# Attention into a bilinear MLP on one core: the order of one transpose, and of two exponentials behind a copy

## The chip, the cores and the metric

The kernel runs on one core of a Trainium2 chip. The metric is the device time of the whole program in microseconds. Times are medians of several executions; the profile is of one further execution with the hardware profiler.

## The reference

Two stages are chained. Both work in float32 (the MLP weights come as float64 and are converted).

```python
# attention, B=8 batches, H=8 heads, S=512 tokens, Ns=32 state rows, D=64
scores  = x @ state.T / 8;  a  = softmax(scores,  over the 32 state rows);  xread = a  @ state
scores2 = state @ x.T / 8;  a2 = softmax(scores2, over the 512 tokens);     sread = a2 @ x
y = concat([xread, sread], tokens).reshape(B * (S + Ns), H * D)
# MLP without activations
out = (((y @ w1) * (y @ w2)) @ w3) @ w_out
```

Both softmaxes read the same scores, once in each direction: for the token reads a maximum over 32 state rows belongs to each token, for the state reads a maximum over 512 tokens belongs to each state row.

## The kernel before

**Tiles.** The scores of a batch are computed with the 8 x 32 state rows of all heads on the partitions: a PSUM tile of 128 x 2 x 512 (two banks, `per_head` at line 148, called by `scores` at line 183). The hidden layer of a batch has eight tiles of 128 features (`ft` 0 to 7). For each, `stage1_sums` (line 320) makes 12 matmuls of 512 columns into a PSUM tile of two banks; ScalarE copies the first bank to SBUF (line 524) and VectorE multiplies the copy with the second bank (line 403, in `hidden_quarters`). All of these two-bank tiles, those of the scores among them, come from one pool, `ps_2`, with three buffers. A matmul group that takes a buffer waits until everything that reads its former content is done.

**Order in a batch.** `quarter_batch(b)` runs the hidden layer of batch b and, beside it, the softmaxes of batch b+1. TensorE's order is written by hand: tiles 0 and 1, then the last piece of state weights (line 148), the state read of batch b (line 252), the scores of batch b+1 (line 148), then tiles 2 to 7, and then the products of the second layer (lines 434 to 451). With three buffers in turn, tile 4 takes the buffer of the scores, so it waits for all that reads them.

**What reads the scores** is in `scores` (lines 180 to 206):
- `turn`, line 191: VectorE transposes the whole tile in blocks of 32 x 32 into SBUF, for the softmax over state rows. That goes on with a maximum (line 213), a subtraction (line 214) and an exponential (line 217) on the SBUF copy.
- `maxima`, lines 194 and 195: VectorE takes the maximum of each row over the 512 tokens, then multiplies the small result (128 x 2) with -1/8.
- the exponentials, line 204: ScalarE, one for each of the two banks, with the scaled maxima as bias and the row sums accumulated; each is followed by a short instruction that reads the accumulator.

For batches above `PLAIN` (= 1) the program traces maxima first, then the transpose; for batches 0 and 1 the other way round.

**What sets the order of the engines.** TensorE and SyncE issue in program order throughout, ScalarE and VectorE only in the prologue, to which the softmaxes of batch 0 belong (they end in lines 626 to 630). Everywhere else a planner orders ScalarE and VectorE at compile time: it walks through a modelled time and gives a free engine the ready instruction that comes first by priority (program order; what stands under `high_priority`, the copies of line 524 and the products of line 403, goes before the rest). On the chip each engine then works its list strictly in that order. `tc.issue_after(i)` adds an order to the plan: what its block traces on the engine of `i` is queued behind `i`. It adds no wait on other engines.

The planner also sets the waits between engines. For PSUM it keeps instructions of two engines on the same bank apart, also when both only read it. In the program as compiled, the first exponential of batch 2 waits for the count that the transpose of batch 2 raises, though it uses nothing that the transpose makes. Batch 2 is the only batch whose transpose stands behind the scaled maxima in VectorE's list; in batches 3 to 7 the multiplication stands last, and the exponential waits for its count.

The calls in `quarter_batch` that drive this, at tile 2:

```python
            elif ft == 2:
                next(softmax, None)
                with tc.issue_after(q["whole"].ins):
                    next(softmax, None)
```

The first `next` traces the transpose, the maxima and the exponentials, the second lines 213 to 217, which stand on VectorE behind the product of tile 2 (line 403).

Of the kernel before, what the change touches and what calls it, by code (L numbers as in the profile page):

```python
# [36 lines left out]
PLAIN = 1  # L37

@with_exitstack
def attn_bilinear_kernel(  # L40
# [10 lines left out]
    nc = tc.nc  # L51
# [10 lines left out]
    SCALE = 1.0 / math.sqrt(D)  # L62
# [26 lines left out]
    def bank():  # L89
        return ps_o.tile([P, NF], F32, name="ps_o")  # L90

    def two_banks():
        return ps_2.tile([P, 2, NF], F32, name="ps_2")

    def split(hi, lo, src):

        return (
            nc.scalar.copy(out=hi, in_=src),  # L98
            nc.vector.tensor_tensor(out=lo, in0=src, in1=hi.bitcast(F32), op=ALU.subtract),  # L99
        )  # L100
# [41 lines left out]
    def per_head(ps, b, moving):  # L142


        for j in range(NP):
            for q in range(KT):
                rows = slice(q * D, (q + 1) * D)
                nc.tensor.matmul(  # L148
                    ps[j * NS:(j + 1) * NS, q], sts[b][rows, j], moving(rows, j), start=True, stop=True
                )  # L150
# [14 lines left out]
    def work_tile():  # L165
        return att.tile([P, KT, S], F32, name="work")

    def move_blocks(dest, src):

        for j in range(NP):  # L170
            for c in range(P // NS):
                nc.sync.dma_start(
                    out=dest(slice(c * NS, (c + 1) * NS), j), in_=src(slice(j * NS, (j + 1) * NS), c)
                )

    def attention_steps(b):
        xd = x_tiles[b]
        a2 = {}

        def scores():  # L180

            ps = two_banks()
            per_head(ps, b, lambda rows, j: xd[rows, j])
            yield
            flat = lambda t: t.rearrange("p k s -> p (k s)")

            s1 = work_tile()
            m2 = att.tile([P, KT], F32, name="m2")

            def turn():  # L190
                nc.vector.transpose(out=flat(s1), in_=flat(ps))

            def maxima():
                nc.vector.tensor_reduce(out=m2, in_=ps, axis=AX.X, op=ALU.max)
                nc.vector.tensor_scalar_mul(m2, m2, -SCALE)

            for step in (maxima, turn) if b > PLAIN else (turn, maxima):
                step()
            e2 = att.tile([P, KT, S], F32, name="e2", bufs=1)
            sum2 = att.tile([P, KT], F32, name="sum2")  # L200
            a2["e"], a2["sum"] = e2, sum2
            for kt in range(KT):
                one = slice(kt, kt + 1)
                nc.scalar.activation(  # L204
                    out=e2[:, kt], in_=ps[:, kt], func=AF.Exp, bias=m2[:, one], scale=SCALE, accum_out=sum2[:, one]
                )
            if b > PLAIN:
                yield

            J = KT * S // NS  # L210
            s1v = flat(s1).rearrange("p (j n) -> p j n", n=NS)
            m1 = att.tile([P, J], F32, name="m1")
            nc.vector.tensor_reduce(out=m1, in_=s1v, axis=AX.X, op=ALU.max)
            nc.vector.tensor_tensor(
                out=s1v, in0=s1v, in1=m1.unsqueeze(2).broadcast_to([P, J, NS]), op=ALU.subtract
            )
            nc.scalar.activation(out=s1, in_=s1, func=AF.Exp, scale=SCALE)
            yield
            nc.vector.tensor_scalar_add(sum2, sum2, 1e-9)
            nc.vector.reciprocal(out=sum2, in_=sum2)  # L220
            sum1 = att.tile([P, J], F32, name="sum1")
            nc.vector.tensor_reduce(out=sum1, in_=s1v, axis=AX.X, op=ALU.add)
            nc.vector.tensor_scalar_add(sum1, sum1, 1e-9)
            nc.vector.reciprocal(out=sum1, in_=sum1)
            nc.vector.tensor_tensor(
                out=s1v, in0=s1v, in1=sum1.unsqueeze(2).broadcast_to([P, J, NS]), op=ALU.mult
            )
            yield
            at = work_tile()
            nc.vector.transpose(out=flat(at), in_=flat(s1))  # L230
            at_tiles[b] = [att.tile([P, KT, S], F32R, name=f"at_{part}", bufs=1) for part in ("hi", "lo")]
            last = split(*at_tiles[b], at)
            yield

            blocks = work_tile()
            with tc.issue_after(last[1].ins):
                nc.vector.transpose(out=flat(blocks), in_=flat(e2))
            a2["t"] = work_tile() if b < PLAIN else att.tile([P, KT, S], F32, name="e2", bufs=1)
            tiles = lambda t: t.rearrange("p k (t m) -> p (k t) m", m=P)
            move_blocks(lambda its, j: tiles(a2["t"])[its, :, j * NS:(j + 1) * NS],  # L240
                        lambda mine, c: tiles(blocks)[mine, :, c * NS:(c + 1) * NS])

        def read_state():

            xs = token_tiles[b]

            ps = (bank() if b else two_banks()[:, 0])[:, :KT * D].rearrange("p (k d) -> p k d", k=KT)
            for kt in range(KT):
                for t in range(NT):
                    for j in range(NP):  # L250
                        mine = slice(j * NS, (j + 1) * NS)
                        nc.tensor.matmul(  # L252
                            ps[mine, kt], a2["t"][:, kt, t * P + j * NS:t * P + (j + 1) * NS],
                            xs[:, t, 2 * j + kt], start=(t == 0), stop=(t == NT - 1),
                        )
            scaled = att.tile([P, KT, D], F32, name="scaled", bufs=1)
            a2["read"] = nc.vector.tensor_tensor(
                out=scaled, in0=ps, in1=a2["sum"].unsqueeze(2).broadcast_to([P, KT, D]), op=ALU.mult
            )
            turned = att.tile([P, KT, D], F32, name="turned")  # L260
            nc.vector.transpose(
                out=turned.rearrange("p k d -> p (k d)"), in_=scaled.rearrange("p k d -> p (k d)")
            )
            yield
            move_blocks(lambda its, j: sread[its, j, b * NS:(b + 1) * NS],
                        lambda mine, c: turned.rearrange("p k (c n) -> p (k c) n", n=NS)[mine, c])

        return scores, read_state, a2


# [40 lines left out]
    def stage1_sums(b, ft):  # L311
        half, c = divmod(ft * P, NF)
        ps = two_banks()
        hi, lo = at_tiles[b]
        for i in range(2):
            w_hi, w_lo = sw_tiles[b][half, i]
            k = 0
            for kt in range(KT):
                for w, a in ((w_hi, lo), (w_hi, hi), (w_lo, hi)):
                    nc.tensor.matmul(  # L320
                        ps[:, i], w[:, kt, c:c + P], a[:, kt], start=(k == 0), stop=(k == 3 * KT - 1)
                    )
                    k += 1
        return ps
# [59 lines left out]
    def tmp_tile():  # L384
        return main.tile([P, NF], F32, name="tmp", bufs=4)
# [131 lines left out]
    def quarter_batch(b):  # L517
        q = {"raw": []}
        softmax = iter(())
        for ft in range(FT):  # L520
            ps = stage1_sums(b, ft)
            a_sb = tmp_tile()
            with tc.high_priority():
                nc.scalar.copy(out=a_sb, in_=ps[:, 0])  # L524
            hidden_quarters(a_sb, ps[:, 1], ft, q)
            if ft == 1:
                run([*late_units, reads[b]])
                if b + 1 < B:
                    scores, reads[b + 1], _ = attention_steps(b + 1)
                    softmax = scores()  # L530
                    next(softmax)
                    load_tokens(b + 1)
                if b + 2 < B:
                    load_x(b + 2)
            elif ft == 2:
                next(softmax, None)
                with tc.issue_after(q["whole"].ins):
                    next(softmax, None)
            elif ft == 4:
                next(softmax, None)  # L540
            if b == PLAIN and ft == 1:
                combine_weights(QF - 1)
        units = sw_steps(b + 1) if b + 1 < B else []
        late_units[:] = units[3:]
        stage2_quarters(b, q, units[:3], [lambda: softmax])

    def run(steps):
        for step in steps:
            for _ in step() or ():
                pass  # L550


    with tc.tile_pool(name="pro", bufs=2) as pro:
# [62 lines left out]
        softmax = scores()  # L616
# [136 lines left out]
```

## Time and profile before

| | |
|---|---|
| median of 3 runs | 497.06 us (496.87 to 497.6) |
| the profiled execution | 496.86 us, span of its instructions 495.1 us |
| around the span | 1.76 us |
| TensorE busy | 483.6 us (98% of the span) |
| VectorE busy | 389.6 us (79%) |
| ScalarE busy | 236.0 us (48%) |
| mean granted TensorE clock | 0.999 |

The profile names an instruction by line, engine (PE TensorE matmul, PEld its weight load, DVE VectorE, ACT ScalarE, SP SyncE), operation and tiles. In the timeline a row has its start, its duration, and in brackets the idle time of its engine ahead of it with what ended that. Starts are in microseconds from the start of the span. Instructions of one engine are pipelined, so that the next one can start a little before the end of the one ahead; what a chain pays for an instruction is mostly the distance from start to start.

### The profile page before, as it was taken

What the parts mean: (1) busy time and instruction counts of PE and PEld (TensorE: products, weight loads), DVE (VectorE), ACT (ScalarE), POOL (GpSimd) and SP (SyncE); (2) the same over time, 40 slices, a digit from 0 to 9 for tenths busy, and PEclk for the clock granted to TensorE, in tenths of its full rate; (3) what the DMA queues carried; (4) which work ended last, traced back from release to release, by engine and by line L of the source; (5) the groups of instructions that cost most, each with busy time, mean ns of one, the idle gap of its engine ahead of it and who ended that gap; (6) DMA issues with size and microseconds to landing.
All of it is one profiled execution on the core that took longest, in us unless ns stands there. A gap on an engine that the chain in (4) does not pass through costs nothing.

```text
span 495.1 us, 8617 instructions
## 1 busy us (share of the span) xinstructions
PE 483.6 (98%) x3390; PEld 368.8 (74%) x3390; DVE 389.6 (79%) x576; ACT 236.0 (48%) x364; POOL 0.2 (0%) x4
## 2 busy tenths in 40 slices
PE   8999999999999999999999999999999999999996
PEld 5444467767788868886888688767976797899885
DVE  5669896799899579958995898589858985678870
ACT  4777784454456045604560455045504551454640
POOL 0000000000000000000000000000000000000000
PEclk9999999999999999999999999999999999999999
DMA  8996971053114404130413041304130223001101
GB/s 339 363 377 235 373 277 28 16 218 61 34 42 164 105 4 177 41 89 5 177 41 90 5 178 43 86 5 178 44 86 5 88 44 85 6 3 42 44 1 44
DMA packets 56361, 52.49 MB, mean 106 GB/s; under 512 B 42752, under 2 KB 50944, under 8 KB 51712
## 3 DMA queue, kind: packets, MB, share of 16 engines
q1 hardware_dynamic: 47488, 43.27, 26.3%
q10 hardware_dynamic: 8832, 8.65, 5.1%
q8 instruction: 27, 0.44, 0.4%
q14 instruction: 14, 0.11, 0.1%
HBM read 38.27 MB, written 8.91 MB: 95 GB/s over the span
## 4 chain that ended last, share of the span: by engine, by line
PE 88%; ACT 4%; DVE 3%; issue 3%; DMA 1%; ACTq 0%; DVEq 0%
PE ps L320 32%; PE ps_o L434 11%; PE ps L446 8%; PE ps L148 7%; PE ps_o L334 7%; PE ps_o L439 5%; PE ps L451 4%; PE ps L691 3%; PE ps_o L584 3%; PE ps_o L571 3%; PE ps L571 3%; PE ps L693 2%; PE ps_o L252 1%; ACT e L204 1%; DMA raw<-in_w_k_dram 1%
## 5 line engine op out<-in xcount | busy, mean ns | idle before, releaser
L320 PE MATMUL ps<-at_lo,sw_hi 128*128 128x512 f32 x256 | 101.9, 398 | 4.8 <-ACT e L204 4.8
L320 PE MATMUL ps<-at_hi,sw_hi 128*128 128x512 f32 x256 | 99.9, 390 | 0.0
L320 PE MATMUL ps<-at_hi,sw_lo 128*128 128x512 f32 x256 | 99.8, 390 | 0.0
L524 ACT COPY tmp<-ps 128x512 f32<-128x512 f32 x56 | 32.8, 585 | 112.9 <-PE ps L320 101.5
L320 PEld LDWEIGHTS ps<-at_lo,sw_hi 128*128 128x128 f32 x256 | 48.1, 188 | 22.9 <-ACT e L204 7.3
L320 PEld LDWEIGHTS ps<-at_hi,sw_lo 128*128 128x128 f32 x256 | 48.1, 188 | 10.2
L320 PEld LDWEIGHTS ps<-at_hi,sw_hi 128*128 128x128 f32 x256 | 48.1, 188 | 9.6 <-issue 0.2
L403 DVE TENSOR_TENSOR g_x<-tmp,ps 128x512 f32<-128x512 f32 x28 | 19.2, 686 | 34.6 <-ACT tmp L524 34.6
L462 DVE TENSOR_TENSOR tmp<-tmp,ps 128x512 f32<-128x512 f32 x42 | 28.9, 687 | 19.0 <-PE ps L451 18.1
L99 DVE TENSOR_TENSOR sw_lo<-ps,sw_hi 128x1024 fp32r<-128x1024 f32 (+1 forms) x34 | 38.3, 1147 | 1.5 <-ACT sw_hi L98 1.5
L98 ACT CAST g_hi<-raw 128x512 fp32r<-128x512 f32 x42 | 24.5, 618 | 16.9 <-DVE raw L403 9.1
L98 ACT CAST g_hi<-g_x 128x512 fp32r<-128x512 f32 x42 | 26.0, 622 | 12.4 <-PE ps_o L434 6.3
L434 PEld LDWEIGHTS ps_o<-t,g_hi 128*128 128x128 f32 x224 | 27.7, 191 | 5.5 <-issue 5.0
L148 PE MATMUL ps<-w_sb,st 64*32 64x512 f32 (+1 forms) x544 | 31.4, 571 | 0.0
L98 ACT CAST sw_hi<-ps 128x1024 fp32r<-128x1024 f32 (+1 forms) x34 | 31.1, 966 | 0.5 <-PE ps L148 0.5
L434 PE MATMUL ps_o<-t,g_hi 128*128 128x256 f32 x224 | 29.8, 286 | 0.3 <-ACT tmp L482 0.3
L99 DVE TENSOR_TENSOR g_lo<-raw,g_hi 128x512 fp32r<-128x512 f32 x42 | 28.2, 685 | 1.9 <-PE ps_o L439 1.6
L434 PE MATMUL ps_o<-wo,g_hi 128*128 128x256 f32 x224 | 29.1, 283 | 0.0
L434 PEld LDWEIGHTS ps_o<-wo,g_hi 128*128 128x128 f32 x224 | 28.3, 192 | 0.5
L584 PE MATMUL ps_o<-w_sb,w 128*128 128x512 f32 x64 | 28.5, 599 | 0.0
L99 DVE TENSOR_TENSOR g_lo<-g_x,g_hi 128x512 fp32r<-128x512 f32 x42 | 27.1, 681 | 1.8 <-PE ps_o L439 1.8
L446 PE MATMUL ps<-t,g_hi 128*128 128x512 f32 x112 | 28.1, 393 | 0.0
(103 smaller groups left out, 784.7 us busy)
## 6 DMA issues: line engine op xcount, KB each, us to landing
raw<-in_w_k_dram SPq DMA_DIRECT2D x8, 1024.0 KB, 6.9
x_d<-in_x_d_dram SPq DMA_DIRECT2D x8, 1024.0 KB, 7.2
raw<-in_w_dram SPq DMA_DIRECT2D x8, 1024.0 KB, 6.2
x_s<-in_x_s_dram SPq DMA_DIRECT2D x8, 1024.0 KB, 5.0
out_dram<-tmp ACTq DMA_DIRECT2D x56, 128.0 KB, 1.9
raw<-in_w3t_dram SPq DMA_DIRECT2D x4, 1024.0 KB, 7.2
e<-work SPq DMA_DIRECT2D x112, 32.0 KB, 2.0
sread<-turned SPq DMA_DIRECT2D x128, 4.0 KB, 1.7
```

Of the source, the lines that this page charges most:

```text
L98: nc.scalar.copy(out=hi, in_=src),
L99: nc.vector.tensor_tensor(out=lo, in0=src, in1=hi.bitcast(F32), op=ALU.subtract),
L148: nc.tensor.matmul(ps[j * NS:(j + 1) * NS, q], sts[b][rows, j], moving(rows, j), start=True, stop=True)
L320: nc.tensor.matmul(ps[:, i], w[:, kt, c:c + P], a[:, kt], start=(k == 0), stop=(k == 3 * KT - 1))
L334: nc.tensor.matmul(ps[:, :DO], g, wo[w][:, ft, :], start=(ft == 0 and k == 0), stop=(ft == FT - 1 and k == 2))
L434: nc.tensor.matmul(ps[:, tt * HO:(tt + 1) * HO], g, w(part, k), start=(fresh and k == 0 and tt == 0 and part == "lo"), stop=False, skip_gr ...
L439: nc.tensor.matmul(ps[:, tt * HO:(tt + 1) * HO], g, w("hi", k), start=False, stop=(k == QF - 1), skip_group_check=True)
L446: nc.tensor.matmul(ps[:, tt].rearrange("p (n d) -> p n d", n=2), g, w(k), start=(k == 0), stop=False, skip_group_check=True,)
L462: sum2 = lambda out, x, y: nc.vector.tensor_tensor(out=out, in0=x, in1=y, op=ALU.add)
L524: nc.scalar.copy(out=a_sb, in_=ps[:, 0])
L571: nc.tensor.matmul(w34_ps[i][:, :DO], chunks[k][:, DO + i * P:DO + (i + 1) * P], w_out[k], start=(k == 0), stop=(k == FT - 1),)
L584: nc.tensor.matmul(w34_ps[i][:, :DO], w3s[i][:, k * P:(k + 1) * P], w_out[k], start=(k == 0), stop=(k == FT - 1))
```

## The change

In `scores`, the second of the two steps is queued on VectorE behind the last instruction of the first: for batches above `PLAIN` the transpose behind the scaled maxima, for batches 0 and 1 the two instructions of the maxima behind the transpose. In `quarter_batch`, what the softmax traces on ScalarE at tile 2, the two exponentials of line 204, is queued behind ScalarE's copy of that same tile, the third.

```diff
             def turn():
-                nc.vector.transpose(out=flat(s1), in_=flat(ps))
+                return nc.vector.transpose(out=flat(s1), in_=flat(ps))
 
             def maxima():
                 nc.vector.tensor_reduce(out=m2, in_=ps, axis=AX.X, op=ALU.max)
-                nc.vector.tensor_scalar_mul(m2, m2, -SCALE)
-
-            for step in (maxima, turn) if b > PLAIN else (turn, maxima):
-                step()
+                return nc.vector.tensor_scalar_mul(m2, m2, -SCALE)
+
+            first, second = (maxima, turn) if b > PLAIN else (turn, maxima)
+            with tc.issue_after(first().ins):
+                second()
...
             with tc.high_priority():
-                nc.scalar.copy(out=a_sb, in_=ps[:, 0])
+                copied = nc.scalar.copy(out=a_sb, in_=ps[:, 0])
...
             elif ft == 2:
-                next(softmax, None)
+                with tc.issue_after(copied.ins):
+                    next(softmax, None)
                 with tc.issue_after(q["whole"].ins):
                     next(softmax, None)
```

## The prediction

> **What bounds the kernel now.** I read the page's head first, then the waits of TensorE, then the timeline of the stretch in which those waits lie.
>
> ```profile
> span 495.1 us, 8617 instructions
> PE 483.6 (98%) x3390; PEld 368.8 (74%) x3390; DVE 389.6 (79%) x576; ACT 236.0 (48%) x364; POOL 0.2 (0%) x4
> ```
>
> TensorE is the engine that sets the end, and only what it waits for can be won. The view of the waits, for TensorE, is led by one line that comes back (total, times, longest):
>
> ```profile
> PE ps L320 <- ACT e L204: 4.8, 5, 1.0
> ```
>
> Five times tile 4 of the hidden layer stands still for ScalarE's exponentials, about 1 us each. The five are the same event in five batches, those that compute the scores of batches 3 to 7; I follow the first of them. TensorE's timeline there:
>
> ```profile
> 181.64 0.39 PE L320 MATMUL ps<-at_hi,sw_hi 128*128 128x512 f32 x1
> 181.87 0.39 PE L320 MATMUL ps<-at_hi,sw_lo 128*128 128x512 f32 x1
> 183.21 0.50 PE L320 MATMUL ps<-at_lo,sw_hi 128*128 128x512 f32 x1 [0.95 <-ACT e L204]
> 183.55 0.40 PE L320 MATMUL ps<-at_hi,sw_hi 128*128 128x512 f32 x1
> 183.79 0.39 PE L320 MATMUL ps<-at_hi,sw_lo 128*128 128x512 f32 x1
> 184.01 0.40 PE L320 MATMUL ps<-at_lo,sw_hi 128*128 128x512 f32 x1
> ```
>
> The step from matmul to matmul is 0.23 (181.64 to 181.87). Without a wait tile 4 would start at 182.10; it starts at 183.21, 1.11 late, and by its fourth matmul the loss is 184.01 - (182.10 + 3 x 0.23) = 1.22, since the pipe fills anew. The last batch, which has no scores to make, checks that; the chain of waits has
>
> ```profile
> 176.59 2.97 PE ps L320 x12
> 183.21 11.17 PE ps L320 x48
> 421.34 16.55 PE ps L320 x72
> ```
>
> The same 72 matmuls of tiles 2 to 7 take 16.55 there, and 183.21 + 11.17 - 176.59 = 17.79 here: 1.24 more. So the whole stall is worth 5 x 1.24 = 6.2 us, and no version of this change can win more. What keeps tile 4 waiting is read from ScalarE and VectorE:
>
> ```profile
> 181.23 0.69 ACT L204 ACTIVATE e<-ps,m 128x512 f32<-128x512 f32 x1 [4.28 <-issue]
> 181.81 0.19 ACT L204 ACTIVATION_READ_ACCUMULATOR e<-ps,m 128x1 f32 x1
> 181.90 0.57 ACT L524 COPY tmp<-ps 128x512 f32<-128x512 f32 x1
> 182.37 0.70 ACT L204 ACTIVATE e<-ps,m 128x512 f32<-128x512 f32 x1
> 182.95 0.21 ACT L204 ACTIVATION_READ_ACCUMULATOR e<-ps,m 128x1 f32 x1
> 183.04 0.59 ACT L524 COPY tmp<-ps 128x512 f32<-128x512 f32 x1
> ```
>
> ```profile
> 178.75 1.19 DVE L194 TENSOR_REDUCE m<-ps 128x2 f32<-128x1024 f32 x1
> 179.86 1.23 DVE L191 STREAM_TRANSPOSE work<-ps 128x1024 f32<-128x1024 f32 x1
> 181.01 0.13 DVE L195 TENSOR_SCALAR m<-m 128x2 f32<-128x2 f32 x1
> 182.51 0.69 DVE L403 TENSOR_TENSOR g_x<-tmp,ps 128x512 f32<-128x512 f32 x1 [1.37 <-ACT tmp L524]
> 183.12 1.21 DVE L213 TENSOR_REDUCE m<-work 128x32 f32<-128x1024 f32 x1
> 184.24 0.16 DVE L219 TENSOR_SCALAR sum<-sum 128x2 f32<-128x2 f32 x1
> 184.36 1.22 DVE L214 TENSOR_TENSOR work<-work,m 128x1024 f32<-128x1024 f32 x1
> ```
>
> The chain is: maximum (178.75), transpose (179.86), scaling (181.01), first exponential (181.23), the copy of the third tile (181.90), second exponential (182.37), end of its accumulator read (183.16), tile 4 (183.21). The scaling needs only the maximum, but stands behind the transpose. The copy has been possible since the third tile's matmuls ended, at 176.59 + 2.97 = 179.56, while ScalarE sat idle for 4.28 with the exponential at the head of its queue, and is now paid for between the two exponentials.
>
> **Part 1: the copy goes ahead of the exponentials.** ScalarE is free from 181.23 - 4.28 = 176.95, so the copy runs at about 179.6 to 180.2, in a time in which ScalarE does nothing. Between the exponentials it goes away. What two exponentials in direct succession cost stands in batch 2:
>
> ```profile
> 134.27 0.58 ACT L524 COPY tmp<-ps 128x512 f32<-128x512 f32 x1
> 134.75 0.69 ACT L204 ACTIVATE e<-ps,m 128x512 f32<-128x512 f32 x1
> 135.33 0.20 ACT L204 ACTIVATION_READ_ACCUMULATOR e<-ps,m 128x1 f32 x1
> 135.42 0.69 ACT L204 ACTIVATE e<-ps,m 128x512 f32<-128x512 f32 x1
> ```
>
> From start to start 135.42 - 134.75 = 0.67, against 182.37 - 181.23 = 1.14 now. That takes 0.47 off the path. Behind the copy on ScalarE waits nothing but the exponentials, which can't run before 181.2 anyway. The cover is wide: the copy would cost its 0.47 again only if tile 2 ended after 180.8.
>
> **Part 2: the transpose goes behind the scaling.** Here the order of start is not enough, since it matters what the exponentials wait for. Both exponentials read the banks that the transpose reads, and the planner keeps two engines off one bank: the one compiled instance of the new order, batch 2, has its exponential waiting for the transpose and not for the scaling. So I take it that the exponentials start after the transpose, now the last of the three on VectorE. Then this part doesn't win the transpose's time; it only swaps the two ends of the same chain, and costs a little, because the scaling can't be overlapped with the maximum it needs. No trace here has maximum, scaling and transpose in direct succession; batch 0 has the first two and batch 2 the last two:
>
> ```profile
> 39.33 1.19 DVE L194 TENSOR_REDUCE m<-ps 128x2 f32<-128x1024 f32 x1
> 40.55 0.17 DVE L195 TENSOR_SCALAR m<-m 128x2 f32<-128x2 f32 x1
> ...
> 133.20 0.16 DVE L195 TENSOR_SCALAR m<-m 128x2 f32<-128x2 f32 x1
> 133.27 1.25 DVE L191 STREAM_TRANSPOSE work<-ps 128x1024 f32<-128x1024 f32 x1
> ```
>
> ```profile
> 40.81 0.69 ACT L204 ACTIVATE e<-ps,m 128x512 f32<-128x512 f32 x1 [1.67 <-DVE m L195]
> ...
> 185.62 1.06 ACT L217 ACTIVATE work<-work 128x1024 f32<-128x1024 f32 x1 [1.99 <-DVE work L214]
> ```
>
> Maximum to scaling: 40.55 - 39.33 = 1.22 (lower bound 179.86 - 178.75 = 1.11, the step to an instruction that needs nothing of it). Scaling to transpose: 0.07 (upper bound 0.13, its whole duration). Transpose: 1.23 (1.25 at most). From its end to ScalarE: 185.62 - (184.36 + 1.22) = 0.04 behind a wide instruction, 40.81 - (40.55 + 0.17) = 0.09 behind the scaling; I take 0.08, nearer to the row with the same waiter. The first exponential starts at 178.75 + 1.22 + 0.07 + 1.23 + 0.08 = 181.35, between 181.20 and 181.44; now it is 181.23. So part 2 costs 0.12, at best it wins 0.03 and at worst it costs 0.21.
>
> The page "PSUM — Partial Sum Buffer" of the Trainium skill, section "PSUM bank collisions raise a hardware error", is the rule that speaks against this part: two engines on one bank and the same partitions at once are an error, ScalarE and VectorE both reading included, so software has to keep them apart. In the rows shown here no exponential overlaps its transpose, but none of them tells whether that was the wait or the queue; by this rule the sum is the one below, without it the one of the first rival.
>
> **The sum.** Second exponential 181.35 + 0.67 = 182.02; from its start to tile 4 it stays 183.21 - 182.37 = 0.84; tile 4 starts at 182.86 in place of 183.21. TensorE still waits, 0.76 past 182.10, so the refill stays too and the gain is 0.35 a batch. With the bounds: 181.20 + 0.67 + 0.84 = 182.71 gives 0.50, 181.44 + 0.67 + 0.84 = 182.95 gives 0.26. Five batches: 1.75 us, between 1.3 and 2.5.
>
> **Edits that cost and win nothing.** Batch 0 is ordered by hand, transpose first, as the new edge wants. Batch 1's rows have that order too. Batch 2 has the scaling at 133.20 ahead of the transpose, and its exponentials behind the copy of even the fourth tile (134.27). So up to about 178 us I expect the same lists.
>
> ```profile
> 90.78 1.25 DVE L191 STREAM_TRANSPOSE work<-ps 128x1024 f32<-128x1024 f32 x1 [2.16 <-DMA work<-work]
> 91.95 1.19 DVE L194 TENSOR_REDUCE m<-ps 128x2 f32<-128x1024 f32 x1
> ```
>
> **What is late next.** The product of tile 2 (line 403) waited 1.37 for the copy and starts now behind the transpose, at 178.75 + 1.22 + 0.07 + 1.15 (transpose to scaling, 179.86 to 181.01) = 181.19 in place of 182.51. The softmax behind it (lines 213 and 214) moves 1.3 ahead, more than TensorE's 0.35, so nothing on VectorE becomes late. The copy of the fourth tile follows the exponentials, 0.35 earlier than now. SyncE's order is untouched, and its transfers hang on VectorE and TensorE, which both come earlier. No other wait of TensorE comes back in these batches.
>
> **The rivals.**
>
> First: the exponentials need only the scaling. Then they start at 178.75 + 1.22 + 0.13 + 0.09 = 180.19, the copy's 0.47 from 179.6 being over; the second at 180.86, tile 4 free at 181.70 from ScalarE and at 181.27 from the transpose (180.04 + 1.23). Both lie before 182.10: the stall is gone, 6.2 us, 490.9. For it: the data allow it. Against: the compiled wait of batch 2. 0.06.
>
> Second, slower: the planner puts the copy of the fourth tile between the exponentials. It can't start before 181.87 + 0.39 = 182.26; the second exponential follows at 182.73, tile 4 at 183.57, 0.36 later than now: 5 x 0.36 = 1.8, so 498.9. It decides from the point where the second exponential starts after 182.37. Against: from third to fourth tile TensorE needs 12 x 0.23 = 2.7, copy and both exponentials together 0.47 + 2 x 0.67 = 1.8, so a planner with about these costs has them queued before that copy is due. 0.05. Its sister on VectorE, the product of tile 2 ahead of the transpose, delays that to 179.6 + 0.61 (copy to product, 181.90 to 182.51) + 0.61 (product to line 213) = 180.82 from 180.04, so tile 4 to 183.64: 499.2. In the present lists the copy comes behind the scaling, so its product should come even later than a transpose that is ready at once. 0.04.
>
> Third, no change: the gain of 0.47 is eaten. That needs the first exponential at 181.50 or later, by a longer handover from the transpose, by a step that the planner slips in between scaling and transpose, or by lists of later stages, planned anew from the first difference, that cost TensorE a few tenths a batch. Nothing in the rows points there, but the margin is small: 0.15 a batch. About 497. 0.17.
>
> **How the numbers follow.** The span goes from 495.1 to 493.35, the profiled execution from 496.86 to 495.1. The median of the runs is 0.2 above that execution, so 497.06 - 1.75 = 495.3. The forecast has what is left, 0.68. Its own range is 494.6 to 495.8. A measurement of this kernel can tell about 0.2%, 1.0 us, from no change. Faster by more than that: 0.68 + 0.06 = 0.74; within: 0.17; slower: 0.09. For 8 in 10 the range leaves out 490.9 and the slower cases, 0.15 together, and reaches over most of the third: to 497.1, and down to 494.4 for the scatter of a median.
>
> **What would show it.** Line 194, 195, 191 in this order, starts 1.22 and 0.07 apart. The third tile's copy runs at about 179.6 in the first of the five batches, and no copy stands between the exponentials, which start 0.67 apart, the first 0.1 behind the transpose's end. TensorE's wait for line 204 still five times, 0.6 each in place of 0.95. VectorE's 1.37 for the copy gone. I am wrong if the exponentials overlap the transpose (first rival), if a copy still stands between them, or if a new line shows among TensorE's waits.

## The result and the profile after

| | before | after |
|---|---|---|
| median | 496.97 us (4 runs) | 491.17 us (4 runs) |
| ratio to before | | 0.9879, 95% interval 0.9862 to 0.9897 |
| profiled execution | 496.86 us, span 495.1 | 490.49 us, span 488.7 |

The change makes the kernel 5.8 us faster, 1.2%. I had forecast 495.3 us, in a range from 494.4 to 497.1; the time that came is close to the 490.9 that I gave to the first rival. Two of the ten runs of the experiment `slots_after` took 687.31 and 973.34 us, and no ratio here uses them; the other eight lie between 496.92 and 497.76. Lines below `scores` have moved: the exponentials are at line 205, the matmuls of the hidden layer at 321, the product at 404, the third tile's copy at 525.

The page's head, then TensorE's waits:

```profile
span 488.7 us, 8603 instructions
PE 482.1 (99%) x3390; PEld 368.9 (75%) x3390; DVE 391.0 (80%) x576; ACT 235.5 (48%) x364; POOL 0.2 (0%) x4
```

```profile
PE ps_o L573 <- DVE w_sb L135: 1.0, 1, 1.0
PE ps_o L77 <- DVE work L74: 1.0, 1, 1.0
PE ps_o L435 <- ACT tmp L483: 0.3, 1, 0.3
PE ps L321 <- ACT e L205: 0.2, 1, 0.2
```

The five waits of 1 us are gone, not shortened. The wait of 0.2 that is left for the exponentials is not one of them: it lies at 136.16, in the stretch that makes the scores of batch 2. The chain of waits has tiles 2 to 7 in one piece, in the time that only the last batch needed before:

```profile
176.51 16.55 PE ps L321 x72
```

Before, the same stretch took 17.79. TensorE's timeline has the first matmul of tile 4 at 182.02, one step behind the last of tile 3:

```profile
181.57 0.39 PE L321 MATMUL ps<-at_hi,sw_hi 128*128 128x512 f32 x1
181.80 0.39 PE L321 MATMUL ps<-at_hi,sw_lo 128*128 128x512 f32 x1
182.02 0.39 PE L321 MATMUL ps<-at_lo,sw_hi 128*128 128x512 f32 x1
```

Now the two lists that I had worked out, ScalarE's and VectorE's:

```profile
179.56 0.59 ACT L525 COPY tmp<-ps 128x512 f32<-128x512 f32 x1 [2.68 <-PE ps L321]
181.25 0.69 ACT L205 ACTIVATE e<-ps,m 128x512 f32<-128x512 f32 x1 [1.11 <-DVE work L191]
181.84 0.19 ACT L205 ACTIVATION_READ_ACCUMULATOR e<-ps,m 128x1 f32 x1
181.93 0.68 ACT L205 ACTIVATE e<-ps,m 128x512 f32<-128x512 f32 x1
182.50 0.20 ACT L205 ACTIVATION_READ_ACCUMULATOR e<-ps,m 128x1 f32 x1
182.59 0.58 ACT L525 COPY tmp<-ps 128x512 f32<-128x512 f32 x1
```

```profile
178.68 1.19 DVE L194 TENSOR_REDUCE m<-ps 128x2 f32<-128x1024 f32 x1
179.90 0.17 DVE L195 TENSOR_SCALAR m<-m 128x2 f32<-128x2 f32 x1
179.98 1.24 DVE L191 STREAM_TRANSPOSE work<-ps 128x1024 f32<-128x1024 f32 x1
181.15 0.65 DVE L404 TENSOR_TENSOR g_x<-tmp,ps 128x512 f32<-128x512 f32 x1
```

These lists are as forecast: 1.22 and 0.08 between the three VectorE instructions, the exponential 0.03 behind the end of the transpose and released by it (`<-DVE work L191`), the exponentials 0.68 apart. Their last accumulator read ends at 182.50 + 0.20 = 182.70. But tile 4 starts at 182.02, 0.68 **before** that. Whatever tile 4 writes to, it isn't the buffer that the exponentials are still reading.

The compiled programs say which it is. These are the first PSUM banks of the two-bank tiles in the first of the five batches:

```
            scores  tile 2  tile 3  tile 4  tile 5
before        2       6       4       2       6
after         2       6       4       6       2
```

In the changed program tile 4 takes the buffer of tile 2, which the product at 181.15 + 0.65 = 181.80 sets free, 0.22 ahead of need. The scores' buffer goes to tile 5, whose turn comes at 182.02 + 12 x 0.227 = 184.74.

The kernel before has one batch in which this happens already: batch 2, whose exponentials run from 134.75, behind the copies of the third and the fourth tile. Its trace has the product of tile 2, and the first matmuls of tiles 4 and 5:

```profile
132.27 0.68 DVE L403 TENSOR_TENSOR g_x<-tmp,ps 128x512 f32<-128x512 f32 x1
```

```profile
133.32 0.39 PE L320 MATMUL ps<-at_lo,sw_hi 128*128 128x512 f32 x1
136.25 0.50 PE L320 MATMUL ps<-at_lo,sw_hi 128*128 128x512 f32 x1
```

Tile 4 starts at 133.32, before the first exponential has begun, and 0.37 behind the end of the product of tile 2 (132.27 + 0.68 = 132.95). In the compiled program the two have the same buffer. Tile 5 has that of the scores; it starts at 136.25, behind the exponentials.

### The profile page after: what moved, and what is told of

It reads as the page before. It is cut to its first block, busy times and chain, and to the rows that moved or that the text cites. A ratio compares the mean times of both kernels' runs of the same rounds, so it can differ in the third digit from the quotient of the medians.

```text
span 488.7 us, 8603 instructions
## 1 busy us (share of the span) xinstructions
PE 482.1 (99%) x3390; PEld 368.9 (75%) x3390; DVE 391.0 (80%) x576; ACT 235.5 (48%) x364; POOL 0.2 (0%) x4
## 4 chain that ended last, share of the span: by engine, by line
PE 77%; DVE 7%; SPq 6%; ACT 5%; DMA 3%; issue 1%; ACTq 0%; DVEq 0%
PE ps L321 29%; PE ps_o L435 11%; PE ps L447 8%; PE ps L148 6%; SPq L172 6%; PE ps_o L440 5%; PE ps L452 4%; PE ps L693 3%; PE ps_o L573 3%; PE ps L573 3%; PE ps_o L335 2%; DMA raw<-in_w_dram 2%; PE ps L695 2%; ACT ulps L127 2%; PE ps_o L253 1%
```

## The experiments

The **theory**: the gain is that the copy and with it the product of tile 2 now come ahead of the exponentials, so that the planner gives tile 4 the buffer of tile 2. The **rivals**: the shorter chain of copy and exponentials is the gain whatever the buffer; the assignment of the buffers alone is the gain; the transpose's place has a part in it. To hold the assignment fixed, some kernels name the buffer of every two-bank tile by a list of 137 digits, taken from one of the two compiled programs:

```diff
-        return ps_2.tile([P, 2, NF], F32, name="ps_2")
+        return ps_2.tile([P, 2, NF], F32, name="ps_2" + next(turns), bufs=1)
```

**The new lists with the old buffers** (`slots_before`): the changed kernel, with `turns` from the kernel before.

> The changed kernel, with each two-bank PSUM tile named to the buffer that the kernel before gave it (three tags of one buffer), so tile 4 takes the buffer of the scores again. Buffer theory (the gain is that tile 4 now takes tile 2's buffer): tile 4 waits for the second exponential's accumulator read, 182.70 in the trace of the changed kernel, and starts at 182.75 in place of 182.02; with the refill of 0.12 that is 0.85 a batch, 4.2 in all: 495.4 us, the forecast on record. Rival (the shorter chain of copy and exponentials, and VectorE's lead of 1.3 us, are the gain, whatever the buffer): 491.2 us.

Measured: 495.46 us, ratio 0.9967 (0.9956 to 0.9979). TensorE's wait is back, five times nearly 0.6, and the 0.2 of batch 2 is still there as the sixth; its line of the waits, then tile 4 and ScalarE in the timeline (this trace lies about 0.57 later):

```profile
PE ps L323 <- ACT e L207: 3.1, 6, 0.6
```

```profile
182.37 0.39 PE L323 MATMUL ps<-at_hi,sw_lo 128*128 128x512 f32 x1
183.33 0.50 PE L323 MATMUL ps<-at_lo,sw_hi 128*128 128x512 f32 x1 [0.57 <-ACT e L207]
183.67 0.39 PE L323 MATMUL ps<-at_hi,sw_hi 128*128 128x512 f32 x1
183.90 0.40 PE L323 MATMUL ps<-at_hi,sw_lo 128*128 128x512 f32 x1
184.13 0.40 PE L323 MATMUL ps<-at_lo,sw_hi 128*128 128x512 f32 x1
```

```profile
181.83 0.69 ACT L207 ACTIVATE e<-ps,m 128x512 f32<-128x512 f32 x1 [1.11 <-DVE work L193]
182.42 0.19 ACT L207 ACTIVATION_READ_ACCUMULATOR e<-ps,m 128x1 f32 x1
182.51 0.68 ACT L207 ACTIVATE e<-ps,m 128x512 f32<-128x512 f32 x1
183.08 0.20 ACT L207 ACTIVATION_READ_ACCUMULATOR e<-ps,m 128x1 f32 x1
```

ScalarE works in the same steps as in the changed kernel, the buffer alone is different, and tile 4 starts 0.05 behind the last accumulator read. Without a wait it would start at 182.37 + 0.23 = 182.60, so it is 183.33 - 182.60 = 0.73 late, and 184.13 - (182.60 + 3 x 0.227) = 0.85 by its fourth matmul; before it was 1.22. So the shorter chain alone is worth 0.37 a batch, and the buffer the other 0.85, which is 4.2 us in five batches; by the medians it is 495.46 - 491.17 = 4.3 of the 5.8 us. That rules out the first of these rivals: the shorter chain alone gives about a quarter of the gain.

**The old lists with the new buffers** (`slots_after`): the kernel before, with `turns` from the changed kernel.

> The kernel before, with each two-bank PSUM tile named to the buffer that the changed kernel gives it: tile 4 takes tile 2's buffer, but the lists of ScalarE and VectorE stay as they were. Buffer theory, with the early copy as its condition: the product of tile 2 still ends at 182.51 + 0.69 = 183.20, so tile 4 starts at 183.24 as it did (183.21): 497.1 us. Rival (the assignment of the buffers alone is the gain): 491.2 us.

Measured: 497.29 us, ratio 1.0002 (0.9992 to 1.0012). The wait has its old size and a new name:

```profile
PE ps L322 <- DVE g_x L405: 5.0, 5, 1.0
```

```profile
180.03 1.23 DVE L193 STREAM_TRANSPOSE work<-ps 128x1024 f32<-128x1024 f32 x1
181.19 0.13 DVE L197 TENSOR_SCALAR m<-m 128x2 f32<-128x2 f32 x1
182.68 0.69 DVE L405 TENSOR_TENSOR g_x<-tmp,ps 128x512 f32<-128x512 f32 x1 [1.37 <-ACT tmp L526]
```

```profile
181.40 0.69 ACT L206 ACTIVATE e<-ps,m 128x512 f32<-128x512 f32 x1 [4.28 <-issue]
182.07 0.57 ACT L526 COPY tmp<-ps 128x512 f32<-128x512 f32 x1
```

```profile
183.43 0.50 PE L322 MATMUL ps<-at_lo,sw_hi 128*128 128x512 f32 x1 [0.99 <-DVE g_x L405]
```

Tile 4 waits for the product of tile 2, which ends at 182.68 + 0.69 = 183.37 because its copy (182.07) still ran behind the first exponential. This shows that tile 2's product is what frees the new buffer, and that the assignment alone wins nothing. Both are needed: the early copy, and the buffer that it frees.

**The second half of the change alone** (`copy_only`):

```diff
-                nc.scalar.copy(out=a_sb, in_=ps[:, 0])
+                copied = nc.scalar.copy(out=a_sb, in_=ps[:, 0])
...
-                next(softmax, None)
+                with tc.issue_after(copied.ins):
+                    next(softmax, None)
```

> Only the second half of the change: exponentials behind the third tile's copy, transpose and scaling in the order of before. Buffer theory: the copy runs at 179.6, the product of tile 2 follows the scaling at about 181.1 and ends at 181.8, tile 4 takes that buffer without a wait: 491.2 us. Rival (the place of the transpose has a part in the gain): more than 491.2, up to 495.

Measured: 490.77 us, ratio 0.9875 (0.9860 to 0.9889), the whole gain. VectorE's and ScalarE's timelines, then the first matmul of tile 4:

```profile
178.97 1.18 DVE L194 TENSOR_REDUCE m<-ps 128x2 f32<-128x1024 f32 x1
180.08 1.23 DVE L191 STREAM_TRANSPOSE work<-ps 128x1024 f32<-128x1024 f32 x1
181.23 0.12 DVE L195 TENSOR_SCALAR m<-m 128x2 f32<-128x2 f32 x1
181.27 0.67 DVE L403 TENSOR_TENSOR g_x<-tmp,ps 128x512 f32<-128x512 f32 x1
```

```profile
179.85 0.59 ACT L524 COPY tmp<-ps 128x512 f32<-128x512 f32 x1 [2.68 <-PE ps L320]
181.39 0.69 ACT L204 ACTIVATE e<-ps,m 128x512 f32<-128x512 f32 x1 [0.95 <-DVE m L195]
182.64 0.20 ACT L204 ACTIVATION_READ_ACCUMULATOR e<-ps,m 128x1 f32 x1
```

```profile
182.31 0.39 PE L320 MATMUL ps<-at_lo,sw_hi 128*128 128x512 f32 x1
```

The transpose stands in its old place, and from the maximum to the first exponential it is 181.39 - 178.97 = 2.42, against 181.25 - 178.68 = 2.57 in the whole change: 0.15 less, which tile 4 doesn't feel: it starts behind the product of tile 2 (181.27 + 0.67 = 181.94) and ahead of the end of the exponentials (182.84).

**The first half alone** (`turn_only`): the diff of `scores` without that of `quarter_batch`.

> Only the first half of the change: transpose behind the scaling, nothing about the exponentials and the copy. My prediction's steps would give a loss of 0.12 a batch, 497.6 us, if the copy stays between the exponentials. Buffer theory with a planner that sees the exponentials wait for the transpose: the copy is ready sooner and goes first of itself, the lists are those of the whole change: 491.2 us.

Measured: 491.06 us, ratio 0.9882 (0.9867 to 0.9897), again the whole gain. ScalarE's timeline shows why; the first matmul of tile 4 follows:

```profile
179.96 0.59 ACT L525 COPY tmp<-ps 128x512 f32<-128x512 f32 x1 [2.69 <-PE ps L321]
181.66 0.69 ACT L205 ACTIVATE e<-ps,m 128x512 f32<-128x512 f32 x1 [1.11 <-DVE work L191]
182.91 0.20 ACT L205 ACTIVATION_READ_ACCUMULATOR e<-ps,m 128x1 f32 x1
```

```profile
182.43 0.39 PE L321 MATMUL ps<-at_lo,sw_hi 128*128 128x512 f32 x1
```

The copy is ahead of the exponentials though nothing asks for it, and here too tile 4 starts before they end (183.11). As compiled, both halves alone give all 137 tiles the buffers of the changed kernel. That the copy comes first because the transpose, now last, makes the exponentials ready later in the plan is argued and not shown. So each half does what the other does, and together they are worth no more than one.

**Late exponentials** (`late_exps`): the changed kernel with its own buffers named, and four copies of no use to the result on ScalarE:

```diff
             a2["e"], a2["sum"] = e2, sum2
+            for _ in range(4 if b > PLAIN + 1 else 0):
+                nc.scalar.copy(out=e2[:, 0], in_=xd[:, 0])
```

> The changed kernel, with the buffers named as it has them by itself, and with four extra copies of 512 columns on ScalarE ahead of the exponentials of batches 3 to 7 (into a tile that the first exponential then overwrites). The exponentials start at about 182.6 in place of 181.25 and their last accumulator read ends at about 184.05. Buffer theory: tile 4 does not care, and tile 5, which takes the scores' buffer, starts at 182.02 + 2.72 = 184.74: no wait, 491.2 us. Rival (the chain of the exponentials still sets TensorE's pace): 1.35 a batch, 6.7 in all, 497.9 us.

Measured: 491.15 us, ratio 0.9880 (0.9865 to 0.9895).

```profile
180.11 2.59 ACT L206 COPY e<-x_d 128x512 f32<-128x512 f32 x4
182.60 0.58 ACT L529 COPY tmp<-ps 128x512 f32<-128x512 f32 x1
183.08 0.69 ACT L209 ACTIVATE e<-ps,m 128x512 f32<-128x512 f32 x1
183.66 0.20 ACT L209 ACTIVATION_READ_ACCUMULATOR e<-ps,m 128x1 f32 x1
183.75 0.69 ACT L209 ACTIVATE e<-ps,m 128x512 f32<-128x512 f32 x1
184.33 0.20 ACT L209 ACTIVATION_READ_ACCUMULATOR e<-ps,m 128x1 f32 x1
```

```profile
184.87 0.39 PE L325 MATMUL ps<-at_lo,sw_hi 128*128 128x512 f32 x1
```

The exponentials end at 184.53, 1.8 later than in the changed kernel and 1.4 later than in the kernel before, and cost nothing: this is still ahead of tile 5, which starts 12 matmuls behind tile 4, at 184.87 in this trace. The delay is 0.48 larger than expected: what stands behind the four copies starts at 182.60, where I had the first exponential, but it is the copy of the fourth tile, and the exponential follows at 183.08. The exponentials are off the critical path.

**Naming alone** (`all_named`): as `late_exps`, without the four copies.

> Control: the changed kernel with the buffers named as it has them by itself, nothing else. Every theory: 491.2 us; a difference would be the price of naming the buffers.

Measured: 490.75 us, ratio 0.9874 (0.9858 to 0.9891). Naming the buffers is free, so the two kernels with swapped lists can be read against the unnamed ones.

## Why the prediction was wrong

**What bounds the kernel** was right: the five waits were nearly all of the 6.2 us that I had worked out as the most there is to win (the median fell by 5.8, the span of the profiled execution by 6.4), and no other wait of that size came in their place.

**Part 1 and part 2** were right as chains. From the maximum the first exponential came after 2.57 where I had 2.60; the second followed after 0.68 where I had 0.67. The exponentials do wait for the transpose, 5.3 us in the five batches, 1.11 in the one shown. I had drawn from the Trainium skill's page "PSUM — Partial Sum Buffer", section "PSUM bank collisions raise a hardware error", that software has to keep two readers of one bank apart; the trace agrees, with the first exponential 0.03 behind the end of the transpose. What a collision does, no run here shows.

**The step that failed is the first of the sum**: "tile 4 starts at 182.86", from "from its start to tile 4 it stays 183.21 - 182.37 = 0.84". That took for granted that tile 4 waits for the exponentials in the new program as in the old one, because three buffers go round in turn. `slots_before` is the kernel in which this holds, and there the step was sound: 0.37 a batch where I had 0.35, and a median of 495.46 where I had 495.3. In the changed program the buffers do not go round in those five batches: tile 4 takes the buffer of tile 2 and starts at 182.02, without a wait. They did not go round in all of the old program either, though the section on the kernel before says so of every batch. Batch 2, from which I took the price of two exponentials in succession, has tile 4 at 133.32, ahead of both of them, so the trace that I read already contradicted the premise of this step. I had used the planner for the waits and the order that it sets and forgotten that it hands out the buffers too. Under "What is late next" I even had the product of tile 2 1.3 earlier, at 181.19, without asking what that product sets free.

**The first rival** gave the right number for a wrong reason. It had tile 4 free because the exponentials need only the scaling; they need the transpose, and tile 4 is free because it doesn't need the exponentials. Its time came out right since any way that removes the whole stall is worth the same 6.2; that is luck and no sign for its mechanism.

**The second rival and its sister** did not come up: the copy of the fourth tile follows both exponentials (182.59), and the product follows the transpose (181.15). **The third**, that the gain of 0.47 is eaten, lost its ground with the sum: tile 4 no longer hangs on that gain.

Not anticipated either was that the two parts do the same: I priced them as separate terms, +0.47 and -0.12, where each alone brings the copy forward.

What stays argued is why the planner chooses so. That it takes the buffer that comes free first in its modelled time fits both programs, batch 2 included; no trace shows it.

## What to carry to other kernels

When a matmul group waits for a buffer of a shared pool, ask which buffer it would take if another reader finished first: an order change on the reading engines can hand the group another buffer, and then the whole wait goes and not only the part by which the old reader got shorter. Before costing a shorter chain, list for each buffer of the pool who frees it and when, and check the earliest against the point of need. That buffers go round in turn can be checked in the trace at hand: look for a batch in which the group starts before its supposed readers are done. If a stall's full worth is known (here from a batch without the step), give the case that all of it goes a serious chance, whatever the mechanism.

## What the runs showed of the hardware that I had not expected

ScalarE's four copies from SBUF to SBUF of 512 columns in `late_exps` start at 180.11, 180.77, 181.42 and 182.07, 0.65 to 0.66 apart, each 0.03 behind the end of the one ahead; all four write the same tile. The copy behind the last of them writes another tile and starts 0.53 after it (182.60), before it ends. Copies from PSUM of the same size had steps of 0.47 to 0.48 (181.90 to 182.37 before, 182.60 to 183.08 in `late_exps`). So an instruction that writes where the one ahead writes is not overlapped with it here, and that is the larger part of the difference. The source would be the smaller, by 0.53 against 0.47 to 0.48; no run separates the two, and only this one case was measured.
